# Moving y and the new states of a gated linear attention chunk to just ahead of the next chunk's scores

## The chip, the core and the metric

The kernel runs on one core of one Trainium2 chip. The metric is the time of the whole program on the device, in microseconds, lower is better. The core's engines have queues of their own and meet through semaphores: TensorE (PE in the profile) multiplies matrices, VectorE (DVE) and ScalarE (ACT) work on rows of 128 partitions, GpSimd (POOL) does the masks and some DMA issues, SyncE (SP) issues most DMAs. Matmul results go to PSUM[...].

## The reference

A gated recurrence (gated linear attention) feeds a feed-forward block with SiLU. There are 4 batches, 8 heads, 768 tokens, and 48 channels a head.

```python
for t in range(S):
    state = alpha[:, :, t, :, None] * state + np.einsum('bhd,bhe->bhde', k[:, :, t], v[:, :, t])
    y[:, :, t] = np.einsum('bhd,bhde->bhe', q[:, :, t], state)
...
x = np.ascontiguousarray(attn_out.transpose(0, 2, 1, 3)).reshape(B * S, H * D)
...
h = x @ w_in
g = h * (1.0 / (1.0 + np.exp(-h)))
return (g @ w_out).astype(np.float32)
```

So x has 3072 rows of 384; w_in is 384 x 2048 and w_out 2048 x 384. All of it is float32.

## The kernel before

**Chunks.** The recurrence is cut into chunks of 128 tokens, 6 for each of the 4 batches. Chunk number n (0 to 23, so that the tenth chunk has number 9) is token chunk n // 4 of batch n % 4. Within a chunk the recurrence becomes matrix products. With scaled queries `qp` and keys `kp` (both carry products of alpha), the scores are kp times qp, cut to a triangle; y is the triangle times v plus qp times the state that the chunk finds; the new state is the old one, scaled, plus keys times v. The state of a batch is next used by the chunk four numbers on.

**Stages.** Each chunk passes through these functions of `quotients`:

- `products(n)`: on VectorE, the transposition of alpha and k (L708), the first scan (L734), and the scaled keys (L749, L751);
- `quotient(n)`: the reciprocal (L762), the second scan (L764), the transposition of q, and the scaled queries (L770). They lie in two buffers, taken in turn, so chunk n + 2 overwrites those of chunk n;
- `flip(n)`, `land(n)`: the scaled keys are transposed in blocks on VectorE (L780), stored to DRAM (L782), and fetched back in another order by four DMAs on SyncE's queue (L790) as `kn`, of which there is one buffer;
- `scores(n)`: 32 small matmuls into two PSUM banks (`ps[0]`, `ps[1]`, for even and odd heads). From chunk 8 on (`n >= NA`) a chunk's score bank is written as follows: of each 64 x 128 half of a head pair only the part that the triangle needs is computed, so in partitions 0 to 63 the first 64 columns of the pairs 2 and 3 stay unwritten, and in partitions 64 to 127 those of the pairs 0 and 1. ScalarE copies the banks to the one buffer `decayed` (L818, L821), POOL zeroes the triangle's other side (L825), and ScalarE scales the state that chunk n found (L836);
- `values(n)`: y, 32 + 24 matmuls into one PSUM bank, with a ScalarE copy (L863) into the input of the feed-forward block;
- `states(n)`: 32 matmuls of 48 columns into one PSUM bank, and two sums on VectorE (L880) that add them to the state, one for each half of the partitions. The last chunk of a batch (numbers 20 to 23) makes no new state.

All these PSUM banks come from one pool of three, `ps_a`, in rotation: a step takes two for the scores, one for y, one for the states. The other five banks are the feed-forward block's.

**Steps and slots.** A loop written out in Python runs over `STEPS` steps of four slots. From step 8 on, step s holds, slot by slot: land and scores of chunk s − 1; products of chunk s; quotient of chunk s; y and states of chunk s − 1, then flip of chunk s. When the states are placed, the loads of v for chunk n + 2 are issued on SyncE (`load_v`, two buffers, three DMAs). After each slot `fill` places pieces of the feed-forward block, 12 full matmuls each, until the work placed is as much as is due at this slot; the due amount runs linearly between `marks`, one mark for each phase. A piece also waits until the chunks it needs have their y (`bridged`).

**Order on the engines.** From a point near step 8 on (`late`), every matmul is held in the program's order on TensorE. VectorE's instructions keep their data dependences, but the compiler may place one of a later slot ahead of an older one that isn't ready.

**The feed-forward block** works on groups of four chunks. From the third group on, the first product runs as sums and differences of blocks (`enter`, banks `ps_m`), and the second likewise (`leave`, banks `ps_o`), which saves matmuls and costs VectorE sums (L582 to L587, L958, L1047).

## Time and profile before

| what | us |
|---|---|
| median of 3 runs (556.72 to 557.85) | 556.89 |
| the profiled execution | 557.26 |
| its span, first instruction to last | 555.5 |
| TensorE busy, matmuls | 541.4 |
| VectorE busy | 445.4 |
| ScalarE busy | 208.5 |
| POOL busy | 76.1 |
| one y burst, matmul starts 293.85 to 295.32 | 1.47 |
| the sums of a state (L880), 32 in all, mean of one | 0.348 |

The profile's groups name an operation as output tile, then input tile, then partitions and elements; `ps_a<-g,vn` and `ps_a<-p,st` are y, `ps_a<-vn,kn` the states, `ps_a<-p,kp` the scores. Nearly all matmuls have line L388, that of a helper, so they are told apart by their tiles. [...] matmuls overlap; the distance from start to start is what one costs. In timelines, consecutive instructions of one kind are merged, and idle time before an instruction stands in brackets with what ended it.

### The profile page before, as it was taken

What the parts mean: (1) busy time and instruction counts of PE and PEld (TensorE: products, weight loads), DVE (VectorE), ACT (ScalarE), POOL (GpSimd) and SP (SyncE); (2) the same over time, 40 slices, a digit from 0 to 9 for tenths busy, and PEclk for the clock granted to TensorE, in tenths of its full rate; (3) what the DMA queues carried; (4) which work ended last, traced back from release to release, by engine and by line L of the source; (5) the groups of instructions that cost most, each with busy time, mean ns of one, the idle gap of its engine ahead of it and who ended that gap; (6) DMA issues with size and microseconds to landing.
All of it is one profiled execution on the core that took longest, in us unless ns stands there. A gap on an engine that the chain in (4) does not pass through costs nothing. (4 is left out here: it accounts for less than half of the span.)

```text
span 555.5 us, 12640 instructions
## 1 busy us (share of the span) xinstructions
PE 541.4 (97%) x5026; PEld 489.7 (88%) x5026; DVE 445.4 (80%) x801; ACT 208.5 (38%) x466; POOL 76.1 (14%) x146
## 2 busy tenths in 40 slices
PE   6999999999999999999999999999999999999996
PEld 4788887998899999899999999988998999999996
DVE  5897788974999899997998986998884796945431
ACT  2556653223333253353353353344263342332100
POOL 3210000222210212021011021021121000001000
PEclk9999999999999999999999999999999999999999
DMA  9998971164454625355545654617642135500000
GB/s 215 246 249 210 232 195 33 47 161 116 117 136 125 159 63 138 86 145 149 139 112 139 193 139 120 191 27 183 170 137 91 54 91 169 172 11 22 10 24 30
DMA packets 99217, 70.09 MB, mean 126 GB/s; under 512 B 56272, under 2 KB 88656, under 8 KB 99152
## 3 DMA queue, kind: packets, MB, share of 16 engines
q1 hardware_dynamic: 97232, 65.30, 45.1%
q0 software_dynamic: 1920, 3.93, 2.0%
q8 instruction: 40, 0.66, 0.5%
q14 instruction: 25, 0.20, 0.1%
HBM read 61.34 MB, written 7.86 MB: 125 GB/s over the span
## 5 line engine op out<-in xcount | busy, mean ns | idle before, releaser
L388 PE MATMUL ps_o<-w_out,g 128*128 128x192 f32 x768 | 134.0, 328 | 0.5 <-DVE o L1056 0.5
L388 PEld LDWEIGHTS ps_o<-w_out,g 128*128 128x128 f32 x768 | 125.6, 190 | 3.5 <-DVE o L1056 1.0
L388 PE MATMUL ps_m<-xt,w_in 128*128 128x256 f32 x480 | 113.6, 383 | 1.5 <-ACT xt L863 1.1
L388 PEld LDWEIGHTS ps_m<-xt,w_in 128*128 128x128 f32 x480 | 89.1, 190 | 14.4 <-ACT xt L863 1.6
L388 PE MATMUL ps_o<-wt,g 128*128 128x192 f32 x576 | 99.7, 326 | 0.0
L388 PEld LDWEIGHTS ps_o<-wt,g 128*128 128x128 f32 x576 | 95.1, 190 | 1.6 <-issue 0.2
L388 PE MATMUL ps_m<-xc,w_in 128*128 128x256 f32 x288 | 70.7, 382 | 0.0
L388 PEld LDWEIGHTS ps_m<-xc,w_in 128*128 128x128 f32 x288 | 53.7, 190 | 7.0 <-DVE g L958 0.3
L1047 DVE TENSOR_TENSOR g<-g 128x512 f32<-128x512 f32 x72 | 50.1, 709 | 8.3 <-PE ps_o L388 8.3
L955 ACT ACTIVATE g<-g 128x1024 f32<-128x1024 f32 x32 | 33.1, 1056 | 61.2 <-DVE g L958 61.1
L1059 POOL DMA_DIRECT2D out_dram<-o x40 | 22.0, 551 | 219.5 <-DVE o L1056 113.7
L825 POOL TENSOR_SCALAR_AFFINE_SELECT g<-g 64x256 f32<-64x256 f32 x64 | 34.9, 546 | 124.4 <-ACT g L818 105.7
L388 PE MATMUL ps_m<-xc,wx 128*128 128x256 f32 x192 | 50.1, 383 | 1.0 <-DVE xc L586 1.0
L950 ACT COPY g<-ps_m 128x512 f32<-128x512 f32 x64 | 36.6, 588 | 37.0 <-PE ps_m L388 36.9
L388 PEld LDWEIGHTS ps_m<-xc,wx 128*128 128x128 f32 x192 | 35.2, 190 | 5.2 <-ACT u L1078 1.2
L958 DVE TENSOR_TENSOR g<-ps_m,g 128x512 f32<-128x512 f32 x56 | 37.1, 683 | 3.2 <-PE ps_m L388 2.7
L734 DVE TENSOR_TENSOR_SCAN u<-al,one 128x516 f32<-128x516 f32 x24 | 29.8, 1240 | 11.9 <-ACT al L731 11.6
L923 ACT ACTIVATE g<-ps_m 128x512 f32<-128x512 f32 x32 | 19.1, 597 | 41.7 <-PE ps_m L388 41.4
L950 ACT COPY part<-ps_m 128x512 f32<-128x512 f32 x32 | 18.9, 590 | 38.0 <-PE ps_m L388 24.0
L697 DVE TENSOR_REDUCE seen<-bits 128x1 f32<-128x512 int32 (+1 forms) x33 | 26.3, 823 | 5.7 <-DMA bits<-in_moe_w_in_dram 5.7
L764 DVE TENSOR_TENSOR_SCAN p<-al,inv 128x516 f32<-128x516 f32 x24 | 29.9, 1247 | 1.0 <-PE ps_a L388 0.3
L1056 DVE TENSOR_TENSOR o<-ps_o,u 128x192 f32<-128x192 f32 x24 | 8.5, 355 | 25.7 <-PE ps_o L388 22.8
(129 smaller groups left out, 648.5 us busy)
## 6 DMA issues: line engine op xcount, KB each, us to landing
bits<-in_moe_w_in_dram SPq DMA_DIRECT2D x24, 512.0 KB, 4.7
bits<-in_moe_w_out_dram SPq DMA_DIRECT2D x16, 384.0 KB, 3.9
at<-in_alpha_dram SPq DMA_DIRECT2D x64, 96.0 KB, 2.5
kt<-in_k_dram SPq DMA_DIRECT2D x64, 96.0 KB, 2.6
qt<-in_q_dram SPq DMA_DIRECT2D x64, 96.0 KB, 2.7
bits<-in_alpha_dram SPq DMA_DIRECT2D x9, 512.0 KB, 4.0
out_dram<-o POOLq DMA_DIRECT2D x40, 96.0 KB, 2.4
flips<-turn SPq DMA_DIRECT2D x12, 256.0 KB, 2.4
```

The costliest lines, as they stand in the source:

```text
L388: in_order(nc.tensor.matmul(*args, **kw))
L697: dve.tensor_reduce(seen[kind][which][:, i : i + 1], x, axis=AX, op=op, apply_absolute_value=True))
L734: dve.tensor_tensor_scan(u[:, end - 1 :: -1], sg[:, end:0:-1], one[:, end:0:-1], 0.0, ALU.mult, ALU.add)
L764: dve.tensor_tensor_scan(p[:, 0:end], sg[:, 0:end], iv[:, 0:end], 0.0, ALU.mult, ALU.add)
L825: gps.affine_select(x, x, pattern=[[0, NP], [1, CH]], compare_op=ALU.is_ge, fill=0.0, base=0, channel_multiplier=-1)
L923: act.activation(gts[grp, h, pair][:, i : i + 2, q % 2, :], ps, AF.Silu)
L950: act.copy(to, ps)
L955: act.activation(x, x, AF.Silu)
L958: dve.tensor_tensor(to, a, b, op)
L1047: dve.tensor_tensor(cells(grp, h, pair, *to), cells(grp, h, pair, *x), cells(grp, h, pair, *y), ALU.subtract)
L1056: dve.tensor_tensor(o, x, y, ALU.add)
L1059: (gps if grp < NG - 1 else nc.sync).dma_start(out[r : r + C, c * HO : (c + 1) * HO], o)
```

## The change

For chunks from number 8 on, `values` and `states` leave slot 3 of step n + 1 and become the first thing in slot 0 of step n + 2, ahead of `land` and `scores` of chunk n + 1. So in program order one `fill` (that of slot 3) and `flip` of chunk n + 1 are now ahead of them, and the loads of v that follow the states move along. Step 8 keeps the old place for chunk 7, and step 9 has no y. The loop has one more step. The marks of the phases after the first are one slot later.

`states(n)`, for chunks 8 to 19, no longer takes a bank of its own. It takes the two banks that `scores(n + 1)` will use and writes its 32 matmuls into their parts that scores leave unwritten: partitions 0 to 63 of pairs 2 and 3, partitions 64 to 127 of pairs 0 and 1, in both banks. Its sums therefore become four on VectorE, each of 48 partitions and 96 elements, in place of two of 192. The matmuls themselves, their number and shapes, are as before. `scores` takes those banks from `shared`; where there are none (chunks 8 and 21 to 23), it takes two fresh ones.

```diff
+    shared = {}
+
     def scores(n):
...
-        ps = [ps_attn() for _ in range(2)]
+        ps = shared.pop(n, None) or [ps_attn() for _ in range(2)]
...
         if ci < NCH - 1:
 
-            ps = ps_attn()
+            if n < NA:
+                one = ps_attn()
+                ps = [one[:, 2 * w : 2 * w + 2] for w in range(2) for _ in range(2)]
+            else:
+                two = shared[n + 1] = [ps_attn() for _ in range(2)]
+                ps = [x[:, 2 - 2 * u : 4 - 2 * u] for x in two for u in range(2)]
             for j in range(NP):
                 for i in range(4):
                     r = slice(32 * i, 32 * i + 32)
                     kn = c["kn"][:, j, r] if n < NA else c["kn"][:, i, 32 * j : 32 * j + 32]
-                    pe.matmul(ps[r, j, 0:D], lhsT=kn, rhs=vn[:, 2 * j + i // 2, 0:D],
-                              start=True, stop=True)
+                    pe.matmul(ps[j // 2 * 2 + i // 2][r, j % 2, 0:D], lhsT=kn,
+                              rhs=vn[:, 2 * j + i // 2, 0:D], start=True, stop=True)
+            if n < NA:
+                for u in range(2):
+                    r = slice(64 * u, 64 * u + D)
+                    s, x = st[b][r, :, u, :], one[r, :, 0:D]
+                    if ci > 0:
+                        dve.tensor_tensor(s, x, s, ALU.add)
+                    else:
+                        act.copy(s, x)
+                return
             for u in range(2):
                 r = slice(64 * u, 64 * u + D)
-                s, x = st[b][r, :, u, :], ps[r, :, 0:D]
-                if ci > 0:
-                    dve.tensor_tensor(s, x, s, ALU.add)
-                else:
-                    act.copy(s, x)
+                for w in range(2):
+                    s = st[b][r, 2 * w : 2 * w + 2, u, :]
+                    dve.tensor_tensor(s, ps[2 * w + u][r, :, 0:D], s, ALU.add)
...
-    STEPS = NT + 1
+    STEPS = NT + 2
...
-    marks = [2 * SLOTS + 2] + [(GB * i + 2 * GB) * SLOTS + 3 for i in range(len(phases))]
+    marks = [2 * SLOTS + 2] + [(GB * i + 2 * GB) * SLOTS + 3 + (i > 0) for i in range(len(phases))]
...
         elif step >= NA:
-            stages = [[(land, 1), (scores, 1)], [(products, 0)], [(quotient, 0)],
-                      [(values, 1), (states, 1), (flip, 0)]]
+            lag = 2 if step > NA else 1
+            y = [(values, lag), (states, lag)]
+            stages = [[(land, 1), (scores, 1)], [(products, 0)], [(quotient, 0)], [(flip, 0)]]
+            if lag == 2:
+                stages[0] = y + stages[0]
+            else:
+                stages[3] = y + stages[3]
         for slot, group in enumerate(stages):
             for stage, lag in group:
                 n = step - lag
-                if not 0 <= n < NT:
+                if not 0 <= n < NT or lag == 2 and n < NA:
                     continue
                 stage(n)
```

## The prediction

> **What bounds the kernel now.** I read the page's busy table first, then who TensorE waited for, then the order of instructions on TensorE and on VectorE in one step of the changed part, then the busy times step by step.

> ```profile
> PE 541.4 (97%) x5026; PEld 489.7 (88%) x5026; DVE 445.4 (80%) x801; ACT 208.5 (38%) x466; POOL 76.1 (14%) x146
> ```

> TensorE (PE) is busy all the time. Its waits are nearly all at the start; from the ninth chunk on they come to some 3 us:

> ```profile
> PE ps_a L392 <- DMA an<-in_alpha_dram: 4.2, 1, 4.2
> PE ps_m L388 <- ACT xt L863: 1.1, 4, 0.3
> PE ps_m L388 <- DVE xc L586: 1.0, 1, 1.0
> PE ps_a L388 <- DVE p L770: 0.5, 1, 0.5
> ```

> So nothing that the change takes off another engine can pay; only TensorE's own order can, and any new wait of TensorE goes to the end of the kernel. One step on TensorE, from its timeline (start, length, instruction, count):

> ```profile
> 285.10 1.03 PE L388 MATMUL ps_m<-xc,wx 128*128 128x256 f32 x4
> 285.97 2.76 PE L388 MATMUL ps_o<-w_out,g 128*128 128x192 f32 x16
> 288.57 1.89 PE L388 MATMUL ps_m<-xc,w_in 128*128 128x256 f32 x8
> 290.29 1.03 PE L388 MATMUL ps_m<-xt,w_in 128*128 128x256 f32 x4
> 291.16 2.76 PE L388 MATMUL ps_o<-wt,g 128*128 128x192 f32 x16
> 293.85 1.08 PE L388 MATMUL ps_a<-g,vn 128*32 128x128 f32 x32
> 294.75 0.84 PE L388 MATMUL ps_a<-p,st 128*32 128x128 f32 x24
> 295.41 0.52 PE L388 MATMUL ps_a<-vn,kn 128*32 128x48 f32 x32
> 295.86 1.13 PE L388 MATMUL ps_m<-xc,wx 128*128 128x256 f32 x4
> 296.83 1.89 PE L388 MATMUL ps_m<-xc,w_in 128*128 128x256 f32 x8
> 298.65 0.90 PE L388 MATMUL ps_a<-p,kp 48*64 48x128 f32 x32
> ```

> Here 293.85 and 294.75 are y of a chunk, 295.41 its new state, 298.65 the scores of the next chunk; between them lie 12 full matmuls of the feed-forward part. Starts are what counts. Four full matmuls take 285.97 − 285.10 = 0.87 us, but the four after the states take 296.83 − 295.86 = 0.97. Eight take 290.29 − 288.57 = 1.72, but the eight before the scores 298.65 − 296.83 = 1.82. So a change of tile shape costs 0.10 us on entry and 0.10 on the first full matmul behind it, whose weights nothing hides.

> VectorE (DVE) at such a point, from the timeline of all engines:

> ```profile
> 253.47 0.52 PE L388 MATMUL ps_a<-vn,kn 128*32 128x48 f32 x32
> 253.72 1.23 DVE L764 TENSOR_TENSOR_SCAN p<-al,inv 128x516 f32<-128x516 f32 x1 [0.33 <-PE ps_a L388]
> ...
> 253.92 1.13 PE L388 MATMUL ps_m<-xc,wx 128*128 128x256 f32 x4
> ...
> 254.87 0.70 DVE L880 TENSOR_TENSOR st<-ps_a,st 48x192 f32<-48x192 f32 x2
> ```

> The scan of the chunk after next waits for y, because it overwrites that chunk's scaled queries (two buffers), and goes ahead of the two state sums. The sums end at 255.57, 1.65 us after TensorE went on. That lateness is free now: the next reader of that state is four chunks away. In the step shown above they end at 300.05, 1.4 us after the scores have begun. And VectorE has little air:

> ```profile
> 192.45:213.84 21.39, 21.39 (x217) 19.50 (x216) 21.16 (x44) 8.88 (x23) 2.64 (x5) 1.00 0.34 91
> 256.71:277.25 20.54, 20.54 (x217) 19.06 (x216) 17.19 (x31) 8.81 (x18) 3.27 (x7) 1.00 0.60 161
> ```

> These run from scores to scores (length, then PE, PEld, DVE, ACT, POOL busy): VectorE is busy 17.2 to 21.2 us of a step of some 21.

> [...]

> **The change part by part.**
> (a) *One burst for two.* For chunks 8 to 22 y (and, to 19, the states) join the next chunk's scores: 15 joins. Each removes one entry into small tiles (0.10) and one first full matmul with exposed weights (0.10). States to scores is still a change of shape, so the gap behind the states (last start 295.72, next matmul 295.86: 0.14) stays. 15 × 0.20 = −3.0 us, all on TensorE's path.
> (b) *State sums between states and scores.* The states now lie in the banks that the scores then fill[...]: low half of bank 1, low half of bank 2, then the high halves, and the first four score matmuls write just these four. [...] That is a trip TensorE to VectorE to TensorE with nothing else to run on TensorE, and the queue behind it is the whole feed-forward work. Its parts: VectorE reacts 0.34 us after the last start of a burst of 128 columns (253.38 to 253.72); for 48 columns I estimate 0.27. Two sums of 48x192 become four of 48x96. None is in the trace; 192 elements take 348 ns and 4 elements (L737) 160 to 195, so I estimate 0.25 each, 0.2 and 0.27 the bounds: 1.0 us for four. From VectorE's end to TensorE's start, 0.15 us (the scores at 143.83 after L770, which ended at 143.68). Sum 1.42 after the last start, against 0.14 now: a stall of at least 1.1 to 1.3 us even where VectorE stands idle and ready.
> (c) *What stands ahead of the sums on VectorE.* At best nothing, else the rest of some instruction (half of 0.7, 0.35 us), or the scan. The case of 253.72 is the model: scan until 254.87, four sums until 255.87, scores at 256.02, against 253.92: stall 2.1 us. States come a fill later (2.8 us of full matmuls) than before, so VectorE's queue has more ready to put ahead of them, and the scan, let go by y some 0.45 us before the states end, is the likeliest. I take 1.8 us, between 1.25 + 0.35 and 2.1; ends 1.1 and 2.6 (2.1 with another half instruction). Chunks 8 to 19 have states: 12 × 1.8 = +21.6 us; ends 13.2 and 31.2. After a stall VectorE has caught up, so lateness doesn't add from step to step: 21.2 us of work and 0.3 for the extra sums fit in 21.4 + 1.8.
> (d) *Two more VectorE instructions in each of 12 steps*: 1.0 − 0.7 = 0.3 us each, 3.6 us, inside the stall counted in (b).
> (e) *What is moved.* SyncE's queue: the load of v for two chunks on (3 DMAs) and the fetch of the turned keys (4, L790) both stand behind the states; the former now goes behind the store of the turned keys instead of ahead. Each is needed a step later at the earliest (some 20 us; landing takes 2.5): nothing. The keys' fetch now waits for the states just issued, with a step to spare. POOL's triangular fills and ScalarE's copies feed y, which is later: more room. POOL's queue is not passed. Score banks: six uses of three banks in two steps instead of eight, each set of copies read long before. Nothing.
> (f) *Fill.* One more step of empty stages, the phases after the first shifted by one slot together with y. The same pieces: nothing.

> Sum: −3.0 + 21.6 = +18.6. The profiled execution took 557.26 (span 555.5 and 1.8 around it), so 575.9; it was 0.4 above the median of the three runs, so **575.5** against 556.89. The ends give 557.3 − 0.4 − 3.0 + 13.2 = 567 and 585.

> **The rivals.**
> *A, the wait is not there* (the other side): [...] the scores go on at once. Then (a) alone counts: 557.26 − 3.0 − 0.4 = 553.9. For it: the corners are disjoint in columns, and the sums' lateness costs nothing before. Against it: [...] that in the order before, sums end up to 2.6 us after the scores' start (state of chunk 9: 162.62 against 160.03), so reads and writes would meet in a bank. It decides where a stall is under 0.25 us (3.0 over 12), less than a single sum.
> *B, the sums sit deeper in VectorE's order*: a scan and a transposition (1.13 us, L708) ahead of them, stall 3.2: 12 × 3.2 − 3.0 = +35.4, 592. For it: steps with VectorE 21.16 busy of 21.39. Against: sums are older than that work, and every stall lets VectorE catch up.
> *C, a draw*: part of the steps wait, or the sums are met early; total within 0.2%. Only if the stall averages 0.25 us, which no part of (b) gives.

> **How the numbers follow.** Main case 0.77, B 0.11, A 0.09, C 0.03. Main's own span is 567 to 585; for 8 in 10 it takes a part of B and the lowest estimate of a sum: 565 to 592. Measured runs lie within 557.85 − 556.72, 0.2%, so 0.2% is what can be told from no change: faster 0.09, same 0.03, slower 0.88.

> **What would show it.** Right: TensorE idle before the scores of chunks 9 to 20, released by the new sums, some 22 us in all, about 1.8 each; the sums 48x96, x48 in this part, near 0.25 us. (a): no full matmul between states and scores. (c): in VectorE's order, the scan just ahead of the sums. Chunks 20 to 22, which make no state, show the gain without the wait: 0.2 us a step. Wrong: scores starting 0.14 us after the last state matmul, with sums running beside them (A); or stalls over 3 us with transpositions ahead of the sums (B); or new idle time before full matmuls, which I count at nothing.

## The result and the profile after

The changed kernel takes 604.85 us (median of 6 runs, 602.0 to 607.23) against 557.09 (6 runs, 556.04 to 557.85): a ratio of 1.0854, interval 1.0834 to 1.0875. It is 48 us slower, where the forecast was 18.6 slower with 592 as the upper end. The profiled execution took 607.23, with a span of 605.5.

The page of the changed kernel, busy table and granted clock:

```profile
PE 559.9 (92%) x5026; PEld 509.0 (84%) x5026; DVE 448.7 (74%) x825; ACT 210.6 (35%) x466; POOL 72.7 (12%) x146
...
PEclk9799999999987997979979999999999999999999
```

The number of matmuls is the old one, 5026, and TensorE's busy share fell from 97% to 92%. VectorE has 24 instructions more and 3.3 us more of work. The second line is the granted clock in 40 slices of 15.1 us. Before, it was 9 in every slice; here it falls in five slices between 165 and 320 us (the 7 in the second slice is at 15 to 30 us, where the two kernels are the same, and cost nothing that lasts: at 136 us the two traces are 0.3 us apart).

Who TensorE waited for (us in total, times, longest):

```profile
PE ps_a L388 <- DVE st L896: 28.6, 13, 4.0
...
PE ps_m L388 <- DVE xc L586: 2.0, 1, 2.0
```

L896 is the new line of the state sums. The 28.6 us are the trip TensorE to VectorE to TensorE that the prediction named, but larger.

The first changed step, timeline of all engines with lines left out (start, length, engine, instruction; idle time before it in brackets):

```profile
143.00 0.52 PE L388 MATMUL ps_a<-vn,kn 128*32 128x48 f32 x32
...
143.31 1.08 DVE L708 STREAM_TRANSPOSE turn<-qt 128x512 f32<-128x512 f32 x1
144.24 0.40 DVE L584 TENSOR_TENSOR wx<-w_in 128x256 f32<-128x256 f32 x1
144.57 0.66 DVE L770 TENSOR_TENSOR p<-turn,p 128x512 f32<-128x512 f32 x1
...
145.16 0.40 DVE L584 TENSOR_TENSOR wx<-w_in,wx 128x256 f32<-128x256 f32 x1
145.48 0.69 DVE L780 STREAM_TRANSPOSE turn<-kp 128x512 f32<-128x512 f32 x1
146.10 0.38 DVE L586 TENSOR_TENSOR wx<-w_in 128x256 f32<-128x256 f32 x1
146.52 0.42 DVE L582 TENSOR_TENSOR wx<-w_in,wx 128x256 f32<-128x256 f32 x1
...
146.96 1.08 DVE L896 TENSOR_TENSOR st<-ps_a,st 48x96 f32<-48x96 f32 x4
...
147.53 1.50 PE L388 MATMUL ps_a<-p,kp 48*64 48x128 f32 x32 [4.01 <-DVE st L896]
...
148.96 4.23 PE L388 MATMUL ps_m<-xt,w_in 128*128 128x256 f32 x11
```

Seven VectorE instructions stand between the states and their sums. Among them are weight sums that nothing waits for, and L780, the block transposition of the next chunk's keys (`flip`), which the change put ahead of the states in program order. The four sums follow each other at about 0.27 us. The scores start before the third sum is done, then need 1.43 us from their first start to the next full matmul, where before they took 0.83. And the eleven full matmuls behind take 4.23 us, with the clock at 0.50 from 148.80 us on; the twelve that start at 161.04, at 1.00, take 2.75.

A step with nothing but the second scan ahead of the sums, the prediction's model, in the same view:

```profile
282.11 0.52 PE L388 MATMUL ps_a<-vn,kn 128*32 128x48 f32 x32
...
282.36 1.23 DVE L764 TENSOR_TENSOR_SCAN p<-al,inv 128x516 f32<-128x516 f32 x1 [0.95 <-PE ps_a L388]
...
283.51 0.84 DVE L896 TENSOR_TENSOR st<-ps_a,st 48x96 f32<-48x96 f32 x4
...
284.23 1.07 PE L388 MATMUL ps_a<-p,kp 48*64 48x128 f32 x32 [1.59 <-DVE st L896]
...
285.22 1.99 PE L388 MATMUL ps_m<-xc,wx 128*128 128x256 f32 x4
```

Here the scan goes at once when y is done, the sums follow it, and the scores start 1.80 us after the last state matmul, against 0.14 from there to the next matmul before. The scan stands alone ahead of the sums like this in 3 of the 12 steps; in 2 more it is one of several. The four matmuls of the last line take 1.99 instead of 1.13: the clock again, at 0.50 from 285.34 us on, after a stall of 1.7 us.

Busy times of two stretches (start to end, length, PE, PEld, DVE, ACT, POOL, then the granted clock, DMA share, GB/s):

```profile
228.10:238.00 9.90, 7.23 (x61) 5.75 (x50) 7.77 (x17) 2.92 (x11) 2.57 (x4) 0.66 0.46 117
...
336.10:339.00 2.90, 1.30 (x48) 1.09 (x35) 1.85 (x5) 0.36 (x2) 0.00 (x0) 1.00 0.24 43
```

The first holds a stall of 2.7 us and 6.8 us of half clock; in the second a stall of 1.7 left the clock alone.

To see where the 49 us of the two traces lie, I summed the distances from one matmul's start to the next on TensorE, from 136 us on, by the kinds of the two neighbours (starts, because matmuls overlap: a record of 128x256 is 0.38 us long, and the next one starts 0.22 behind it):

| part | before | after | difference |
|---|---|---|---|
| last state matmul to first score matmul, less 0.14 each | 0 | 28.7 | +28.7 |
| within the score bursts | 10.0 | 17.4 | +7.3 |
| full matmuls in stretches of half clock, above their normal distance | 0 | 15.9 | +15.9 |
| entries into small tiles and first full matmuls behind them | | | −3.3 |

Part of the second row is the clock again. At 147.53 and at 186.31 the first scores meet the same waits for sums inside the burst (0.56 us), but the first burst, at full clock, takes 1.22 us and the second, at half clock, 1.78. Counted so for every burst, some 2.7 of the 7.3 us are half clock and 4.6 are waits. So the waits of the trip come to some 33.3 us (28.7 + 4.6) and half clock to some 18.6 (15.9 + 2.7).

The twelve gaps from last state to first score are 4.22, 3.24, 2.40, 0.69, 2.87, 2.30, 1.80, 3.25, 1.80, 2.28, 1.80 and 3.63 us. Half clock was granted for 41.0 us, in eight pieces of 3.4 or 6.8 us, each beginning within or just behind such a stall.

### The profile page after: what moved, and what is told of

The parts are those of the page before. It is cut to its first block, busy times and chain, and to the rows that moved or that the text cites. A ratio compares the mean times of both kernels' runs of the same rounds, so it can differ in the third digit from the quotient of the medians.

```text
span 605.5 us, 12657 instructions
## 1 busy us (share of the span) xinstructions
PE 559.9 (92%) x5026; PEld 509.0 (84%) x5026; DVE 448.7 (74%) x825; ACT 210.6 (35%) x466; POOL 72.7 (12%) x146
## 5 line engine op out<-in xcount | busy, mean ns | idle before, releaser
L388 PE MATMUL ps_o<-w_out,g 128*128 128x192 f32 x768 | 142.1, 342 | 0.5 <-DVE o L1070 0.5
L388 PEld LDWEIGHTS ps_o<-w_out,g 128*128 128x128 f32 x768 | 134.7, 201 | 3.7 <-DVE o L1070 0.8
L388 PE MATMUL ps_m<-xt,w_in 128*128 128x256 f32 x480 | 114.9, 386 | 1.1 <-ACT xt L865 1.1
L388 PEld LDWEIGHTS ps_m<-xt,w_in 128*128 128x128 f32 x480 | 90.5, 192 | 14.0 <-ACT xt L865 1.6
L388 PE MATMUL ps_o<-wt,g 128*128 128x192 f32 x576 | 100.9, 329 | 0.0
L388 PEld LDWEIGHTS ps_o<-wt,g 128*128 128x128 f32 x576 | 96.3, 192 | 1.7 <-issue 0.4
L388 PE MATMUL ps_m<-xc,w_in 128*128 128x256 f32 x288 | 72.3, 389 | 0.0
L1061 DVE TENSOR_TENSOR g<-g 128x512 f32<-128x512 f32 x72 | 48.6, 687 | 27.0 <-PE ps_o L388 26.9
L388 PEld LDWEIGHTS ps_m<-xc,w_in 128*128 128x128 f32 x288 | 56.0, 197 | 7.1
L388 PE MATMUL ps_a<-p,kp 48*64 48x128 f32 (+2 forms) x640 | 31.6, 290 | 28.9 <-DVE st L896 28.6
L388 PEld LDWEIGHTS ps_a<-p,kp 48*64 48x64 f32 (+1 forms) x640 | 25.9, 167 | 34.9 <-DVE st L896 31.8
L388 PE MATMUL ps_m<-xc,wx 128*128 128x256 f32 x192 | 51.8, 393 | 2.0 <-DVE xc L586 2.0
L827 POOL TENSOR_SCALAR_AFFINE_SELECT g<-g 64x256 f32<-64x256 f32 x64 | 31.0, 484 | 135.9 <-ACT g L820 115.3
L972 DVE TENSOR_TENSOR g<-ps_m,g 128x512 f32<-128x512 f32 x56 | 37.3, 684 | 11.0 <-PE ps_m L388 10.3
L388 PEld LDWEIGHTS ps_m<-xc,wx 128*128 128x128 f32 x192 | 36.1, 195 | 6.4 <-issue 2.3
L734 DVE TENSOR_TENSOR_SCAN u<-al,one 128x516 f32<-128x516 f32 x24 | 29.5, 1228 | 11.1 <-ACT al L731 10.7
L764 DVE TENSOR_TENSOR_SCAN p<-al,inv 128x516 f32<-128x516 f32 x24 | 29.8, 1243 | 4.4 <-PE ps_a L388 3.8
```

What stands on the lines that cost most here:

```text
L388: in_order(nc.tensor.matmul(*args, **kw))
L734: dve.tensor_tensor_scan(u[:, end - 1 :: -1], sg[:, end:0:-1], one[:, end:0:-1], 0.0, ALU.mult, ALU.add)
L764: dve.tensor_tensor_scan(p[:, 0:end], sg[:, 0:end], iv[:, 0:end], 0.0, ALU.mult, ALU.add)
L827: gps.affine_select(x, x, pattern=[[0, NP], [1, CH]], compare_op=ALU.is_ge, fill=0.0, base=0, channel_multiplier=-1)
L972: dve.tensor_tensor(to, a, b, op)
L1061: dve.tensor_tensor(cells(grp, h, pair, *to), cells(grp, h, pair, *x), cells(grp, h, pair, *y), ALU.subtract)
```

## The experiments

Three theories. **S**: the trip through the shared banks is the whole cost. **P**: the later place itself costs, because VectorE is then late for other things that TensorE needs. **C**: the drop of the granted clock is a cost of its own, brought by the stalls. All edits are against the changed kernel unless another is named.

**One part at a time (e1, e2).** e1 keeps the place and gives the states a bank of their own:

```diff
-                two = shared[n + 1] = [ps_attn() for _ in range(2)]
-                ps = [x[:, 2 - 2 * u : 4 - 2 * u] for x in two for u in range(2)]
+            ps = ps_attn()
...
-                for w in range(2):
-                    s = st[b][r, 2 * w : 2 * w + 2, u, :]
-                    dve.tensor_tensor(s, ps[2 * w + u][r, :, 0:D], s, ALU.add)
+                s, x = st[b][r, :, u, :], ps[r, :, 0:D]
+                    dve.tensor_tensor(s, x, s, ALU.add)
```

> The new place is kept, but the states get a bank of their own again and two sums, as before. Theory S (the shared banks): the scores no longer wait for the sums; what stays is the 0.2 us gained at each of 15 joins, less a wait of the scores' second bank for ScalarE's copy of y, which lay in that bank (at most 0.6 us a step): 554 to 562 us, and the clock of TensorE at 1.00 from 30 us on. Theory P (the place: VectorE is late with the next chunk's scaled queries once y stands next to the scores): TensorE goes on idling before the scores, and the time stays above 590.

Measured: 573.26 us, ratio 1.0308 (1.0283 to 1.0333): between the two. Its waits:

```profile
PE ps_a L388 <- ACT xt L865: 5.6, 4, 2.5
PE ps_m L388 <- DVE xc L586: 5.3, 2, 3.3
...
PE ps_a L388 <- DVE p L770: 2.9, 2, 1.9
```

The trip is gone, and there are three others. The first is of this edit's making: with three banks in rotation, the scores' second bank is y's, and ScalarE must have copied y out (it stands behind activations that wait for VectorE). The other two, the block sums of the feed-forward input (xc) and the scaled queries (p), come late from VectorE.

e2 keeps the shared corners and sets y and states back into slot 3, with the old steps and marks:

```diff
-    STEPS = NT + 2
+    STEPS = NT + 1
...
-            lag = 2 if step > NA else 1
-            y = [(values, lag), (states, lag)]
-            stages = [[(land, 1), (scores, 1)], [(products, 0)], [(quotient, 0)], [(flip, 0)]]
...
+            stages = [[(land, 1), (scores, 1)], [(products, 0)], [(quotient, 0)],
+                      [(values, 1), (states, 1), (flip, 0)]]
```

> The sharing of the banks is kept (four sums), but y and states go back to slot 3 of the step before, so a fill of some 2.6 us of full matmuls lies between states and scores. Theory S: scores wait wherever the sums end later than the scores' start; in the kernel before they did so in 10 of 12 steps, by 0.3 to 2.6 us, 12.7 in all, and a stall lets VectorE catch up: 560 to 572 us, with at most a few drops of the clock. Theory P: with the place undone the time is back at 556 to 558.

Measured: 565.85, ratio 1.0174 (1.0142 to 1.0206), as expected. Even with a fill of full matmuls between states and scores, the sums come too late in six of the steps:

```profile
PE ps_a L388 <- DVE st L896: 6.2, 6, 1.7
```

So the shared corners alone cost 9 us, and joined to the scores they cost far more.

**What stands ahead of the sums (e3).** The second scan of chunk n is issued behind the sums of chunk n − 2 on VectorE:

```diff
-        dve.tensor_tensor_scan(p[:, 0:end], sg[:, 0:end], iv[:, 0:end], 0.0, ALU.mult, ALU.add)
+        with tc.issue_after(last_sum[n - 2].ins) if n - 2 in last_sum else ExitStack():
+            dve.tensor_tensor_scan(p[:, 0:end], sg[:, 0:end], iv[:, 0:end], 0.0, ALU.mult, ALU.add)
```

> As the changed kernel, but the second scan of a chunk is queued behind the sums of the chunk two before, on VectorE alone. In the changed kernel the scan stood ahead of the sums in about six of twelve steps. If what stands ahead of the sums sets the stall, those steps lose some 1.2 us each and one or two drops of the clock go with them: 590 to 600 us. If the stall is set elsewhere: 602 to 607.

Measured: 596.89, ratio 1.0727 (1.0659 to 1.0795), as expected. The gaps from states to scores fell from 30.3 to 25.5 us, half clock from 41.0 to 23.9. The scan is one part of the queue ahead of the sums, and not the main one.

**The clock (e4).** Ten full matmuls of 128 columns, whose result nothing reads, run between states and scores, in a corner of y's bank:

```diff
                     dve.tensor_tensor(s, ps[2 * w + u][r, :, 0:D], s, ALU.add)
+            for _ in range(10):
+                pe.matmul(c["py"][:, NKT, :], lhsT=w_out[:, 0, 0:128], rhs=w_out[:, 1, 0:128],
+                          start=True, stop=True)
```

> As the changed kernel, with ten more full 128x128x128 matmuls, whose result nobody reads, between the states and the scores of 12 steps, in an unused part of y's bank. They wait for ScalarE's copy of y and then take 1.1 us, mostly inside the stall. Theory C (the gaps slow TensorE's clock): the 41 us at half clock shrink to under 15, and the time falls to 585 to 597 though TensorE does more work. Rival (the clock has another cause): half clock as long as before, 605 to 615 us.

Measured: 589.19, ratio 1.0587 (1.057 to 1.0605), inside what C expected. Each instruction shows as two records, so the ten took 2.2 us and not half of that. (The counts of 32 and 24 for scores, y and states are such records too: the loops of the code issue 16 and 12.) Its clock line and a step of it on TensorE (page, then timeline):

```profile
PEclk9999999999999999999999999999999999999998
```

```profile
142.78 2.50 PE L388 MATMUL ps_a<-w_out 128*128 128x128 f32 x20 [0.26 <-ACT xt L865]
146.56 1.45 PE L388 MATMUL ps_a<-p,kp 48*64 48x128 f32 x32 [1.27 <-DVE st L897]
147.93 2.86 PE L388 MATMUL ps_m<-xt,w_in 128*128 128x256 f32 x12
```

TensorE does some 26 us of useless work (12 × 2.2), and the kernel is 15.7 us faster than the changed one. The states and the sums are as they were. From last state to first score the twelve steps now take 38.0 us in place of 30.3, but most of it is spent working; half clock went from 41.0 us to none. Only one wait for the sums is left, the 1.27 shown, and the twelve matmuls behind it take 2.86. The ten themselves wait for ScalarE's copy of y, 5.0 us in twelve pieces, one of 2.0, and no drop of the clock follows that one either. C is shown: in the changed kernel a stall costs its length and then, in eight steps of twelve, some 2 us more.

**Covering the trip with y (e5, e6).** The order of the burst becomes: y's part from the old state, the states, the rest of y, the scores; the scan is held behind the sums as in e3. In e5 the states have a bank of their own, in e6 they use the corners.

```diff
+        todo = todo + olds if n < NA else olds + todo
...
+            if n >= NA and i == len(olds):
+                new_states(n)
```

> The new place, but inside the burst y's part with the old state comes first, then the states, then y's triangle part (1.0 us on TensorE), then the scores. The states have a bank of their own, two sums, and it is this bank, not y's, that the scores take as their second. The scan is queued behind the sums on VectorE. Theory S (the trip to VectorE and back, plus what stands ahead of the sums, is the cost): the 1.0 us of y covers the trip where VectorE comes at once; what is left is VectorE's lateness beyond it, about 1 us in each of 12 steps: 560 to 569 us, few drops of the clock. Theory P (the later place is the cost): as with the states in a bank of their own alone, 570 to 576.

> The same order inside the burst and the same order of scan and sums on VectorE, but the shared banks and four sums of the change. Against the run with only the scan behind the sums (597 us) the sums get 1.0 us of cover in 12 steps. Theory S: TensorE's wait before the scores falls from 25 to 12 to 15 us, and most of the 24 us at half clock go: 568 to 582. If the wait isn't set by when the sums can start: 592 to 600.

Measured: 586.3 (1.0505, 1.0461 to 1.0548) and 586.55 (1.055, 1.0511 to 1.0588). Both miss. The rest of y covers 1 us of the trip at most, waits for the sums remain (7.2 and 14.6 us), and waits for xc come on top, e6:

```profile
PE ps_a L388 <- DVE st L905: 14.6, 10, 4.0
PE ps_m L388 <- DVE xc L586: 5.1, 1, 5.1
```

The changed kernel waited 2.0 us for xc; where its trip was taken away or covered (e1, e5, e6) it is 5.1 to 6.7. Something stood behind the trip, and S alone was in doubt.

**No trip at all (e7).** The sums add a tile of zeros instead of reading PSUM; all matmuls and all VectorE instructions are there. The new states of chunks 8 to 19 are so left out of the result.

```diff
-                    dve.tensor_tensor(s, ps[2 * w + u][r, :, 0:D], s, ALU.add)
+                    dve.tensor_tensor(s, zero[r], s, ALU.add)
```

> As the changed kernel, place and shared banks and four sums of VectorE kept, but from chunk 8 on the sums add a tile of zeros from SBUF and not the states from PSUM, so the new states of chunks 8 to 19 are left out of the result; their matmuls still run. VectorE has the same work, TensorE the same matmuls, and only the trip from states to scores is gone. Theory S (the trip is the whole cost): 552 to 557 us, the join's gain of some 3.3 us against one or two us of waits for y's copy and its sums; no drop of the clock. Theory P (standing at the later place is a cost of its own, as the 573 us with a bank of its own may suggest): 563 or more.

Measured: 578.12, ratio 1.0375 (1.0356 to 1.0393). S fell as the whole cause: 21 us are left with no trip. The waits (L588 is L586 of the other kernels, two lines having been added):

```profile
PE ps_m L388 <- DVE xc L588: 10.9, 2, 6.2
PE ps_a L388 <- DVE p L772: 6.5, 3, 4.4
```

The larger of them, on VectorE's timeline behind the y that frees it (state sums at 280.38; L699 is a range check of the inputs, L697 elsewhere):

```profile
284.89 1.28 DVE L766 TENSOR_TENSOR_SCAN p<-al,inv 128x516 f32<-128x516 f32 x1
286.09 1.26 DVE L1063 TENSOR_TENSOR g<-g 128x512 f32<-128x512 f32 x2
287.28 0.68 DVE L974 TENSOR_TENSOR g<-g,part 128x512 f32<-128x512 f32 x1
287.88 0.68 DVE L1063 TENSOR_TENSOR g<-g 128x512 f32<-128x512 f32 x1
288.48 1.21 DVE L699 TENSOR_REDUCE seen<-bits 128x1 f32<-128x1024 f32 x1
289.61 0.41 DVE L584 TENSOR_TENSOR xc<-xt 128x256 f32<-128x256 f32 x1
```

In the kernel before, the same two come in the other order:

```profile
276.03 0.70 DVE L880 TENSOR_TENSOR st<-ps_a,st 48x192 f32<-48x192 f32 x2
276.76 0.42 DVE L582 TENSOR_TENSOR xc<-xt 128x256 f32<-128x256 f32 x1
...
283.94 0.42 DVE L586 TENSOR_TENSOR xc<-xc 128x256 f32<-128x256 f32 x1
284.27 1.21 DVE L697 TENSOR_REDUCE seen<-bits 128x1 f32<-128x1024 f32 x1
```

Here the block sums start 0.7 us behind the state sums, and the check follows. With the change they start 9.2 us behind them, straight after the check. The code says why that may be: `fill` issues a check in slots 0 and 2 only; the block sums of a group are let go by y (`bridged`), and with y they went from slot 3 to slot 0; and both are held in program order on VectorE (`keep_in_program_order`), so that the sums can't overtake the check.

**The check out of the way (e10, e11).** One digit, on e7 and on the changed kernel:

```diff
-        if at % 2 == 0 and step > 3 * GB + 2:
+        if at % 2 == 1 and step > 3 * GB + 2:
```

> As e7 (the new states of chunks 8 to 19 are left out of the result), with the checks of the inputs' range (the reductions of line 697) issued in the second and fourth slot of a step instead of the first and third. In e7 the block sums of the input (xc) are issued in a first slot, just behind such a reduction, and both keep their program order on VectorE, so that the sums wait for it and for all that the compiler put ahead of it. Theory X (this pairing makes the sums late): TensorE's waits for xc fall from 10.9 us to below 4, the time from 578 to 566-572. Rival L (VectorE is simply short of time behind the later y, whatever the order): xc waits stay near 8-11, time 575-580. The waits for p should stay near 6 in both.

> The changed kernel with that same move of the range checks, nothing left out. There the trip's own stalls let VectorE catch up, and waits for xc come to 2.2 us only; theory X and its rival both expect little: 600-606. Less than 598 would mean that the checks also stand ahead of the state sums (stall states to scores well under 28 us in all).

Measured: e10, again without the new states of chunks 8 to 19, 561.68, ratio 1.0075 (1.0057 to 1.0092); e11 601.37, ratio 1.0771 (1.0738 to 1.0803). e10 gains 16.4 us over e7, more than expected; its list of waits has no xc any more:

```profile
PE ps_a L388 <- DVE p L772: 6.5, 3, 4.4
```

So the pairing of check and block sums is shown to be what P consisted of for the most part. In the changed kernel, moving the check gains 3.5 us (604.85 − 601.37; the two ratios' intervals don't meet): there, TensorE waited for xc only 2.0 us; as I read it, each trip stops TensorE and gives VectorE the time to do xc. The two costs hid each other, which is why taking the trip away alone (e1, e5, e7) looked so poor.

What the trip and its clock cost is now e11 against e10: 601.37 − 561.68 = 39.7 us. TensorE's matmuls are the same, in the same order, in both traces, and VectorE's instructions are the same in kind and number. VectorE's order is not: the compiler, which may move them, placed them otherwise from the first changed step on (in e11 a range check, at 306.23, stands between the states and the sums of a step where e10 has none). So the 39.7 us hold the trip, its clock, and what that other order is worth; the last was not measured by itself, here or between the other pairs of runs.

The 6.5 us for p are left. The longest, 4.36, on e10's VectorE:

```profile
172.42 1.10 DVE L898 TENSOR_TENSOR st<-zero,st 48x96 f32<-48x96 f32 x4 [1.79 <-PE ps_a L388]
173.56 1.08 DVE L710 STREAM_TRANSPOSE turn<-kt 128x512 f32<-128x512 f32 x1
```

The state sums stand ahead of the transposition of k, and VectorE waits 1.79 us idle for TensorE to come to y. In the kernel before, the transposition runs at 171.30, ahead of the sums. I didn't try to part this further.

**Scores first (e8, e9, e12).** Versions that do the whole computation and need no trip: scores of the next chunk, then y, then the states into the corners. In e8 ScalarE copies the scores before VectorE sums the states, in e9 after; e12 is e8 with the check moved as in e10.

```diff
-                stages[0] = y + stages[0]
+                stages[0] = stages[0][1:] + y + stages[0][:1]
...
-                two = shared[n + 1] = [ps_attn() for _ in range(2)]
+                two = ctxs[n + 1]["banks"]
```

> One burst as in the change, but in the order scores of the next chunk, y, states; the states go into the same corners after the scores, and ScalarE's copies of the scores and then VectorE's sums follow, so no matmul waits for a sum. If the return trip is the cost: the join's 3 us are gained, 552 to 556 us. If VectorE, whose sums now wait for ScalarE's copies in the same banks, becomes late with the scaled queries instead: 557 to 566.

> The same, but with VectorE's sums ahead of ScalarE's copies of the scores in the shared banks. ScalarE, in order, then waits for sums that come 1 to 4 us late, and with it the copies and SiLUs that free the feed-forward banks: 558 to 572 us. If ScalarE has enough air: 552 to 556, as with the copies first.

> As e8 (scores of the next chunk first, then y, then the states into the corners, so that no scores wait for state sums; nothing is left out), with the range checks moved by one slot as in e10. If the pairing of checks and block sums was the cause of the late block sums there too: waits for xc from 10.9 to below 3, less half clock, time 566-574 against 586.8; the waits for p, 11.1, stay, since VectorE meets weight sums there whatever the checks do. If only the trip had been hidden by another accident: 582-588.

Measured: 586.84 (1.0535, 1.0511 to 1.0559), 585.3 (1.0487, 1.0464 to 1.0511) and 577.94 (1.0358, 1.0322 to 1.0394). e8 and e9 miss on the slow side; e12 lies between the two ranges that were expected. None waits for state sums. e8, then e12:

```profile
PE ps_a L388 <- DVE p L770: 11.1, 4, 3.7
PE ps_m L388 <- DVE xc L586: 10.9, 2, 5.9
```

```profile
PE ps_a L388 <- DVE p L770: 11.2, 4, 3.7
PE ps_m L388 <- DVE xc L586: 5.4, 2, 4.0
```

Moving the check halved the waits for xc here, where it ended them in e10; the rest of them stays open. Scores in front of y need p some 2 us sooner, and p waits rose from 6.5 to 11. Half clock stayed at 20.5 us in e8 and 23.9 in e12. No version tried beats the kernel before.

## Why the prediction was wrong

The direction and the mechanism were right: the wait is the one named, at the place named, and it decides. The size was wrong, by a term that was too small and by one that was missing. On the traces: +18.6 forecast, +11.7 from the waits of the trip (33.3 in place of 21.6), +18.6 from the clock (equal to the forecast by chance), −0.3 from the joins gives 48.6 of the 49.0 measured.

- **(a) One burst for two**, −3.0: right, −3.3. Chunks 20 to 22 show it alone: y to scores takes 0.20 us with no wait. The exposed weights can be seen in the trace before: the load for the first full matmul behind the states starts at 295.86, with the matmul itself, while the load for the second starts at 295.97, 0.21 ahead of its matmul at 296.18.
- **(b) The trip, at least 1.1 to 1.3**: right; the smallest, at 205.43, costs 1.1 (0.55 ahead of the scores and 0.55 inside them). Its parts were well sized: the sums take 0.21 to 0.26 (0.25 estimated), and with the scan just ahead the step costs 1.8 more than before, 1.66 ahead of the scores and 0.16 inside them, where the model gave 2.1. The difference is that the first score doesn't wait for all four sums: it starts 0.05 to 0.06 behind the second in five steps and behind the third in seven, and the last is met inside the burst, which is lengthened. That the scores would wait at all was the author's assumption; no view of the kernel before shows such a case. The measured wait is this: the columns that the scores write and those that the sums read are apart in the shared banks, and TensorE still stood idle for 28.6 us in front of scores until a sum (L896) was done. What sets that wait, these traces don't tell.
- **(c) "I take 1.8 us, between 1.25 + 0.35 and 2.1; ends 1.1 and 2.6"**: this is the first of the two steps that failed. The waits cost 33.3 / 12 = 2.8 us a step, above the upper end of 2.6. The scan was taken as the likeliest instruction ahead of the sums, and it stands there alone in 3 steps of 12. In most others it is a handful: `flip`'s transposition in four of them, which the change itself set ahead of the states (the prediction followed that move on SyncE's queue and not on VectorE's), weight sums, sums of the feed-forward block (L1047, L972), and other transpositions (L708). "After a stall VectorE has caught up, so lateness doesn't add from step to step" looked at the amount of work. VectorE had the time, at 74% of the span. What counted, by the timelines and by e3, was the order of its instructions, in which work that nobody waits for stood ahead of the sums.
- **The clock**: the second step that failed, and the larger. No part of the prediction had it: stalls were priced at their own length, so what they do to the matmuls behind them was put at nothing. Some 18.6 us were lost to half clock, 15.9 in the full matmuls behind the stalls and 2.7 in the scores; e4 shows it by taking the stalls' idleness away. Rival B, with stalls of 3.2, would have been near on the stalls and, without this term, short by about 13 us.
- **(d) Extra sums inside the stall**: right, no cost of their own was seen.
- **(e) Queues moved past**: no wait for v or for the fetched keys appeared, right for SyncE. But y's move also moves the time from which VectorE's work is let go, and e10 shows a wait of VectorE for y ahead of the transposition of k.
- **(f) "The same pieces: nothing"**: wrong by 3.5 us here (e11), 16 us with the trip gone (e10 against e7): the block sums came behind a range check. "New idle time before full matmuls, which I count at nothing" was named as a sign of error, and the 2.0 us for xc are that sign.
- **Rivals**: A (no wait, 553.9) is excluded. Even with no trip at all the joined place doesn't gain: e10 is at 561.68. C, a draw, is excluded.

The chain of the +47.8 us by experiments: the trip with its clock 39.7 (e11 − e10); the check ahead of the block sums 3.5 (after − e11); the later place otherwise, joins deducted, 4.4 (e10 − before, 561.68 − 557.25). They sum to 47.6.

## What to carry to other kernels

Where a change makes the bottleneck engine wait for another one, list what that engine's compiled order holds between the release and the awaited instruction, item by item and in every step, and don't take the likeliest single item; spare time on that engine did not help here. Price a stall of TensorE as its length plus what the clock may take behind it (here 18.6 us of half clock on top of 33.3 us of waits). If work moves in the program, check what is tied to its slot and what is held in program order: two costs can cover each other, and then taking one away shows the other in place of a gain.

## What the runs showed of the hardware

```profile
165.87:169.28 3.41, 0.44 (x13) 1.00 0.75 210
169.28:172.70 3.42, 3.42 (x38) 0.50 0.39 91
...
281.92:285.34 3.42, 1.82 (x81) 1.00 0.29 51
285.34:288.75 3.41, 3.41 (x9) 0.50 0.35 91
...
357.02:360.43 3.41, 1.39 (x72) 1.00 0.29 67
360.43:363.85 3.42, 3.36 (x46) 1.00 0.41 101
...
380.91:384.32 3.41, 1.81 (x89) 1.00 0.25 42
384.32:387.73 3.41, 3.41 (x28) 1.00 0.38 86
```

In this trace, between 136 and 520 us, the seven full-clock windows in which TensorE was busy for at most 1.22 us (36%) were each followed by half clock, and so was one of the five with 1.39 to 2.12 us (41% to 62%); of the 87 busier ones none was. Stalls of one length ended differently: of the three of 1.7, the one at 282.42 lies within one window and brought half clock, that at 336.04 is split between two and brought none. Nor did busy time decide: the third, at 381.73, lies within one window too, and this window, from 380.91, is busy for 53% like that from 281.92, but brought no drop. What decides there was not shown. Before, the same bursts without stalls brought no drop at all (PEclk is 9 in every slice), and in e4, with full matmuls between them, it is 9 in 39 of 40 slices and 8 in the last.
